# Opening loads of a gated linear-attention and token-MLP kernel: two x tiles moved to Pool's queue, PE's order adapted to it

## Chip, cores, metric

One core of one Trainium2 chip. The metric is device time in microseconds (us). The kernel before takes 165.78 us (median of 6 runs, 165.58 to 165.94). One execution of each kernel was also profiled. Its span, 163.6 us for the kernel before, runs from the first to the last recorded instruction and is some 2 us shorter than the device time. Times inside an execution count from the start of the span.

Engine names are those of the profile: PE (TensorE), PEld (its weight loads), DVE (VectorE), ACT (ScalarE), POOL (GpSimd), SP (SyncE). SP, ACT and Pool can each issue DMA. A queue of one of these engines carries a "q" (SPq). In the DMA parts of the profile, q1 hardware_dynamic is SP's queue, q10 is ACT's, and q0 software_dynamic is Pool's.

## The reference

Condensed from the full program:

```python
def reference(A_x, A_wqkv, A_wo, B_x, B_w1, B_b1, B_w2, B_b2, gate_w):
    x = A_x                                            # 1 x 2048 x 512, bf16
    g = sigmoid((x * gate_w).sum(-1, keepdims=True))
    a = linear_attention(x, A_wqkv, A_wo)              # 32 heads of 16
    b = token_mlp(layernorm(x), B_w1, B_b1, B_w2, B_b2)  # mixes over S, F = 1792
    return g * a + (1 - g) * b
# linear_attention: q, k, v = x @ wqkv; phi(t) = where(t > 0, t + 1, exp(t)) + 1e-6;
# kv = phi(k)^T v; z = sum phi(k); o = phi(q) kv / (phi(q) z); o @ wo
```

## The kernel before

x is cut into 16 tiles of 128 rows. The first stage computes K = x Wk tile by tile, and PE needs x transposed for that. Tiles 4 to 15 arrive transposed by DMA (`load_xT`). Tiles 0 to 3 arrive plain and are transposed by PE, so that work can start early. Wk arrives in four chunks of 128 rows, one per `k`.

```python
    load_x(nc.sync, 0, 1)
    load_x(nc.scalar, 1, 1)
    load_wk(nc.sync, 0)
    load_x(nc.scalar, 2, 1)
    load_x(nc.sync, 3, 1)
    for k, q in ((1, nc.scalar), (2, nc.sync), (3, nc.scalar)):
        load_wk(q, k)
    load_xT(4, 2)
    load_xT(6, 2)
    load_x(nc.sync, 4, 4)
    # ... (cut: the other x tiles, Wq, the w1 chunks, Wv, Wo, all on SP)

    nc.gpsimd.memset(ident[:], 0.0)           # identity for PE's transposes, built on Pool
    nc.gpsimd.affine_select(out=ident[:], ...)
    # ... (cut: two masks on Pool)
    warm_up(6)                                # six matmuls on constants, while x is on its way

    HEADS = 4
    transpose_tile(0, False)                  # 4 PE transposes, then a copy on DVE
    transpose_tile(1, True)                   # the same, copy on ACT
    transpose_tile(2, False)
    ln_step(0)
    for k in range(2):                        # six K matmuls on tiles 0 to 2
        for t in range(HEADS - 1):
            k_part(t, (k,))
    transpose_tile(HEADS - 1, True)           # tile 3
    ln_step(1)
    for t in range(HEADS):
        k_part(t, range(2 if t < HEADS - 1 else 0, ND))
        k_phi(t)
```

PE executes its instructions in this order. If one waits, all behind it wait: in the changed kernel below PE idles 2.63 us for one tile while matmuls on three other tiles stand behind the wait.

## Time and profile before

| | before |
|---|---|
| device time, median | 165.78 us |
| PE busy | 159.9 of 163.6 us |
| x0, x1, x2, x3 landed at | 3.37, 3.54, 4.38, 5.70 us |
| first K matmul starts | 4.82 us |
| last PE matmul starts | 160.55 us |
| last output lands | 162.65 us |
| end of span | 163.61 us |

Landings and starts of single instructions are read from the trace.

From the page of the kernel before: the span, the engines' busy times, PE and DMA in 40 slices (tenths busy), and the chain of waits by engine.

```profile
span 163.6 us, 2078 instructions
PE 159.9 (98%) x785; PEld 73.6 (45%) x785; DVE 87.8 (54%) x200; ACT 58.7 (36%) x90; POOL 18.3 (11%) x37
...
PE   7999999999999999999999999999999999999993
...
DMA  5999999999930005800993499932010000111001
...
PE 98%; DVE 0%; issue 0%
```

PE is busy in every slice and the chain is PE alone. The DMA engines are full in the first slices, so loads compete there.

The timeline of PE in the opening of the kernel before (start, length, then what ran; matmuls of one kind are merged):

```profile
3.42 1.62 PE L194 MATMUL pt<-ident,xs 128*128 128x128 bf16 x12
4.82 1.94 PE L108 MATMUL kacc<-wk_sb,xT 128*128 128x512 bf16 x6
6.60 0.39 PE L194 MATMUL pt<-ident,xs 128*128 128x128 bf16 x4
6.83 3.19 PE L108 MATMUL kacc<-wk_sb,xT 128*128 128x512 bf16 x14
```

(The view ends at 13 us.) No line carries an idle time in brackets; a pause of 0.18 us before tile 2's transposes is merged into the first line. Tile 3 landed at 5.70 us and was transposed at 6.60: the six K matmuls in the second line hid its arrival. The fourth line has 14 matmuls in 3.19 us, one every 0.216 us. The first two of the second line started 0.43 us apart. That is the spacing until PE's granted clock rises; this trace holds no clock record.

### The profile page before, as it was taken

To read this page: it belongs to the slowest core of one execution; us is meant where nothing else is said; L and a number is where in the kernel's file an instruction comes from. 1 tells how busy PE (TensorE), PEld (TensorE's weight loads), DVE (VectorE), ACT (ScalarE), POOL (GpSimd) and SP (SyncE) were. 2 spreads that over 40 slices of the span, in tenths; PEclk is the share of its full clock that TensorE was granted. 3 is DMA by queue.
4 is the path that set the end of the run, shared out by engine and by line. 5 is a ranking of instruction groups with operands and counts; after the bars stand their busy time and mean duration, and the time that the engine had idled before them with its cause. 6 is when DMAs were issued, how large, how long until landed. Compare 5 with 4: busy or idle time off the path is not lost.

```text
span 163.6 us, 2078 instructions
## 1 busy us (share of the span) xinstructions
PE 159.9 (98%) x785; PEld 73.6 (45%) x785; DVE 87.8 (54%) x200; ACT 58.7 (36%) x90; POOL 18.3 (11%) x37
## 2 busy tenths in 40 slices
PE   7999999999999999999999999999999999999993
PEld 3444444444544444434444444444444444444452
DVE  0599999958999999109995301156221111111112
ACT  3463386658478373311332113111112222211110
POOL 5000710200200000001055500050000000000000
DMA  5999999999930005800993499932010000111001
GB/s 152 242 243 236 294 300 344 349 348 348 317 78 0 0 0 188 264 0 0 277 303 109 149 289 307 337 126 98 32 36 32 32 32 32 42 50 41 32 32 32
DMA packets 30057, 25.05 MB, mean 153 GB/s; under 512 B 7968, under 2 KB 29472, under 8 KB 30048
## 3 DMA queue, kind: packets, MB, share of 16 engines
q1 hardware_dynamic: 28032, 22.02, 45.5%
q0 software_dynamic: 1440, 2.38, 5.4%
q10 hardware_dynamic: 576, 0.52, 1.1%
q8 instruction: 6, 0.10, 0.2%
q14 instruction: 3, 0.02, 0.0%
HBM read 21.11 MB, written 2.23 MB: 143 GB/s over the span
## 4 chain that ended last, share of the span: by engine, by line
PE 98%; DVE 0%; issue 0%
PE uacc L108 30%; PE yps L108 30%; PE kacc L108 9%; PE aps L108 8%; PE qacc L108 8%; PE gacc L108 8%; PE wps L108 2%; PE pt L194 1%; PE denps L108 1%; PE kvps L108 1%; DVE ot L474 0%; PE zps L108 0%; PE pt L323 0%
## 5 line engine op out<-in xcount | busy, mean ns | idle before, releaser
L108 PE MATMUL uacc<-hs,w1c 128*128 128x512 bf16 x224 | 52.1, 379 | 0.0
L108 PE MATMUL yps<-uT,w2c 128*128 128x512 bf16 (+2 forms) x238 | 51.0, 366 | 0.0
L474 DVE SCALAR_TENSOR_TENSOR ot<-yps,c,a_sc 128x512 bf16<-128x512 f32 (+2 forms) x17 | 12.2, 720 | 45.9 <-PE yps L108 45.8
L108 PEld LDWEIGHTS <-w2c 128*128 128x128 bf16 x238 | 22.8, 98 | 25.9
L108 PEld LDWEIGHTS <-w1c 128*128 128x128 bf16 x224 | 21.7, 98 | 26.0 <-issue 0.4
L461 ACT ACTIVATE a_sc<-aps,c,gg 128x512 f32<-128x512 f32 x16 | 12.4, 778 | 46.7 <-PE aps L108 43.0
L317 ACT ACTIVATE uT<-uacc,bcol 128x512 bf16<-128x512 f32 x14 | 9.3, 687 | 27.7 <-PE uacc L108 27.7
L108 PE MATMUL aps<-W2sb,pqT 128*128 128x512 bf16 x64 | 16.4, 379 | 0.0
L108 PE MATMUL qacc<-xT,wq_sb 128*128 128x512 bf16 x64 | 16.4, 379 | 0.0
L108 PE MATMUL kacc<-wk_sb,xT 128*128 128x512 bf16 x64 | 16.4, 385 | 0.0
L108 PE MATMUL gacc<-pk,xs 128*128 128x512 bf16 x64 | 15.8, 379 | 0.0
L244 ACT ACTIVATE hs<-xs,nmr,rstd 128x512 bf16<-128x512 bf16 x16 | 12.8, 805 | 1.9 <-DVE nmr L238 1.9
L204 ACT ACTIVATE e<-qacc 128x512 bf16<-128x512 f32 x16 | 9.6, 597 | 10.1 <-PE qacc L108 9.2
L413 POOL DMA_DIRECT2D rex<-rd_dram x16 | 9.5, 603 | 23.0 <-DVE pqT L415 18.2
L204 ACT ACTIVATE e<-kacc 128x512 bf16<-128x512 f32 x16 | 9.3, 595 | 6.9 <-PE kacc L108 6.8
L208 DVE SCALAR_TENSOR_TENSOR pk<-kacc,e 128x512 bf16<-128x512 f32 x16 | 11.1, 692 | 0.6
L208 DVE SCALAR_TENSOR_TENSOR pqT<-qacc,e 128x512 bf16<-128x512 f32 x16 | 11.1, 692 | 0.6
L228 DVE BATCH_NORM_STATS2 stats<-xs 128x6 f32<-128x512 bf16 x16 | 10.9, 682 | 0.0
L205 DVE TENSOR_SCALAR e<-e 128x512 bf16<-128x512 bf16 x32 | 9.0, 282 | 3.3 <-ACT e L204 3.3
L400 DVE CUSTOM_DVE_ANT_0 junk<-xs,gw_b 128x512 bf16<-128x512 bf16 x16 | 9.8, 685 | 0.0
L269 DVE TENSOR_TENSOR zacc<-zacc,pk 128x512 f32<-128x512 f32 x14 | 9.6, 686 | 0.2
L108 PEld LDWEIGHTS <-wq_sb 128*128 128x128 bf16 x64 | 6.3, 98 | 7.5
(64 smaller groups left out, 70.1 us busy)
## 6 DMA issues: line engine op xcount, KB each, us to landing
w2c<-in_B_w_dram SPq DMA_DIRECT2D x8, 896.0 KB, 7.5
w1c<-in_B_w_dram SPq DMA_DIRECT2D x2, 2048.0 KB, 15.5
w1c<-in_B_w_dram SPq DMA_DIRECT2D x3, 1024.0 KB, 12.3
rex<-rd_dram POOLq DMA_DIRECT2D x16, 128.0 KB, 2.9
out_dram<-ot SPq DMA_DIRECT2D x15, 128.0 KB, 1.7
xs<-in_A_x_dram SPq DMA_DIRECT2D x3, 512.0 KB, 4.5
wq_sb<-in_A_wqkv_dram SPq DMA_DIRECT2D x1, 512.0 KB, 6.8
wv_sb<-in_A_wqkv_dram SPq DMA_DIRECT2D x1, 512.0 KB, 12.3
```

What stands on the lines that cost most here:

```text
L108: nc.tensor.matmul(o, lhsT=lhsT, rhs=rhs, start=start, stop=stop, **kw)
L204: nc.scalar.activation(out=e[:], in_=acc[:], func=ACT.Exp)
L205: nc.vector.tensor_scalar(out=e[:], in0=e[:], scalar1=1.0, scalar2=PHI_EPS, op0=ALU.min, op1=ALU.add)
L208: nc.vector.scalar_tensor_tensor(out=dst, in0=acc[:], scalar=0.0, in1=e[:], op0=ALU.max, op1=ALU.add)
L228: nc.vector.bn_stats(out=stats[:], in_=xs[:, t, :])
L244: nc.scalar.activation(out=hs[:, t, :], in_=xs[:, t, :], func=ACT.Identity, scale=rstd[:, t : t + 1], bias=nmr[:, t : t + 1],)
L269: nc.vector.tensor_tensor(out=zacc[:], in0=first, in1=pk[:, t, :], op=ALU.add)
L317: nc.scalar.activation(out=uT[:, j, :], in_=acc[:], func=ACT.Gelu_apprx_tanh, bias=bcol[:, j : j + 1])
L400: nc.vector.tensor_tensor_reduce(out=junk[:], in0=xs[:, t, :], in1=gw_b[:], scale=1.0, scalar=0.0, op0=ALU.mult, op1=ALU.add, accum_out=gp ...
L413: nc.gpsimd.dma_start(out=rex[:], in_=src.unsqueeze(1).to_broadcast([8, HEAD, SC]))
L461: nc.scalar.activation(out=a_sc[:], in_=aps[:], func=ACT.Identity, scale=gg[:, t : t + 1], bias=c2[:, t : t + 1],)
L474: nc.vector.scalar_tensor_tensor(out=ot[:, :W], in0=yps[:, :W], scalar=c1[:, t : t + 1], in1=a_sc[:, cs], op0=ALU.mult, op1=ALU.add,)
```

## The change

The intent is to get the opening loads out sooner by using a third queue. x2 and x3 go to Pool's queue, so SP and ACT carry only x0, x1 and Wk. PE then transposes all four tiles before any K matmul, and the w1 chunks 1 and 2 are loaded in halves.

```diff
     load_x(nc.sync, 0, 1)
     load_x(nc.scalar, 1, 1)
-    load_wk(nc.sync, 0)
-    load_x(nc.scalar, 2, 1)
-    load_x(nc.sync, 3, 1)
-    for k, q in ((1, nc.scalar), (2, nc.sync), (3, nc.scalar)):
+    load_x(nc.gpsimd, 2, 1)
+    for k, q in enumerate((nc.sync, nc.scalar, nc.sync, nc.scalar)):
         load_wk(q, k)
@@ (w1 chunks)
-        for t0 in range(0, NT, 8) if c == 0 else (0,):
-            t1 = t0 + 8 if c == 0 else NT
+        for t0 in range(0, NT, 8) if c < 3 else (0,):
+            t1 = t0 + 8 if c < 3 else NT
@@ (after the identity is built on Pool)
+    load_x(nc.gpsimd, 3, 1)
     block_mask(mask[:]...)
@@ (PE's order)
     ln_step(0)
+    transpose_tile(3, True)
+    ln_step(1)
     for k in range(2):
-        for t in range(HEADS - 1):
+        for t in range(HEADS):
             k_part(t, (k,))
-    transpose_tile(HEADS - 1, True)
-    ln_step(1)
     for t in range(HEADS):
-        k_part(t, range(2 if t < HEADS - 1 else 0, ND))
+        k_part(t, range(2, ND))
         k_phi(t)
```

## The prediction

> **What bounds the kernel now.** TensorE. The page has PE busy 98% of a 163.6 us span, and the chain that ended last is 98% PE. In the timeline, matmuls of 512 columns start every 216 ns from about 6.0 us to the last one at 160 us; beyond that spacing I find only some 0.4 us. Only the first 6 us are in play.
>
> There, by the timeline and the DMA landings: x tiles 0 and 1 are issued at 0.80 us and land at 3.4 and 3.5; six warm-up matmuls fill PE from 0.84 to 3.4. Twelve transposes follow at 107 ns each (to 4.8 us), with one pause of 0.18 us for tile 2 (ACT's second DMA, issued 1.24, landed 4.38). Then six K matmuls hide the wait for tile 3 (issued 1.73, landed 5.70), which is transposed at 6.60. Spacing halves (427 to 216 ns) at about 5.6 us: PE is cold before. Real idle in the opening is about 0.25 us.
>
> **What the change does.**
> - x2 goes out on Pool at about 0.8 us. Pool issues in this trace take 0.6 us and land 2.65 us after their start when the queues are quiet: 3.5 to 3.9 us. The 0.18 us pause goes.
> - Pool's identity is built 0.6 us later, about 2.0 us; needed at 3.4. Free.
> - x3 goes out on Pool behind it, at about 2.0 us, later than before (1.73). Pool DMAs beside a bulk load took 3.8 to 4.1 us, and the loads issued around 2 us here 4.0 to 4.6. Estimate: landing at 5.3 to 6.3 us, no sooner than before.
> - The Wk chunks go out up to 0.5 us earlier; none was waited for.
> - SP's first transposing load waits until 3.55 us because its semaphore is that of x tile 1. With two loads fewer on SP and ACT I expect it at 2.2 us, its traffic meeting x3's. The Trainium skill ("DMA: Bandwidth & Descriptors", section "Issuing engines are not separate DMA queues") says all queues share the same 16 engines; DMA is already above 90% busy from 2.5 us here.
> - Tile 3's transpose now stands before all K matmuls. After 12 transposes (4.7 us) it must wait for x3: 0.6 to 1.6 us idle where before six K matmuls ran.
> - Split w1 chunks: before, they land by 48 us and are used later. No gain.
>
> **Sum.** Before, the dense stream starts as if at 6.83 - 6 x 0.216 = 5.53 us; after, at x3's landing plus 0.25: 5.55 to 6.55. That is 0 to +1.0 us. The idle may also hold the clock down: the skill ("TensorE: Matmul & The Clock Gate", Part 1) gives a free-running activity window of about 3.4 us. If the window that ended near 5.4 us no longer counts as busy, PE stays cold up to 3 us longer, costing up to 1.5 us (estimate). I give this one chance in three.
>
> **Prediction.** 166.4 us, 80% range 165.2 to 167.9. Faster by over 2%: 0.01; within 2%: 0.95; slower by over 2%: 0.04.
>
> **What would show it.** A PE wait of 0.6 us or more at the transposes of tile 3, ended by the x DMA; x3 landing after 5.3 us; no pause before tile 2's transposes; the first transposing load issued near 2.2 us; the spacing change at 5.6 us or up to 3 us later; nothing new after 10 us.
>
> **What would make it wrong.** x3 landing before 4.8 us would gain about 0.5 us. Pool's first DMA slowing x0 and x1 would shift everything. A landing after 7 us would exceed the range.

## More of the kernel before

The DMA view of the kernel before (what was loaded, issuing queue, count, KB each, median us from issue to landing), in two stretches: the x tiles issued in the first 3 us, and Pool's loads issued from 17.6 to 19 us, when the DMA engines were full:

```profile
xs<-in_A_x_dram ACTq DMA_DIRECT2D x2, 128.0 KB, 2.9
xs<-in_A_x_dram SPq DMA_DIRECT2D x2, 128.0 KB, 3.3
...
gw_b<-in_gate_w_dram POOLq DMA_DIRECT2D x1, 128.0 KB, 6.9
brow<-in_B_b_dram POOLq DMA_DIRECT2D x1, 3.5 KB, 6.3
brow<-in_B_b_dram POOLq DMA_DIRECT2D x1, 4.0 KB, 6.5
```

The last two lines matter later: on Pool's queue even 4 KB took over 6 us when the engines were full.

## The result, and the profile after

The changed kernel takes 170.94 us (median of 6 runs, 169.72 to 172.39; the longest counts as slow and is left out of the ratio) against 165.78: it is slower, by a ratio of 1.030 (95% interval 1.024 to 1.036). All ratios here are the mean time of one kernel's runs over that of the other's in the same rounds, so not quite the ratio of the quoted medians. Executions over 1.5% slower than the fastest of the same kernel are left out of the means. The prediction was 166.4 us, so it was 4.5 us too low.

From the page of the changed kernel, the lines that answer to those above:

```profile
span 169.4 us, 2066 instructions
PE 161.6 (95%) x771; PEld 74.2 (44%) x785; DVE 87.7 (52%) x200; ACT 58.7 (35%) x90; POOL 19.4 (11%) x39
...
PE   7399999999999999999999999999999999999992
...
PE 93%; DMA 3%; issue 1%; POOL 1%; DVE 0%; POOLq 0%
```

PE's second slice (4.2 to 8.5 us) fell from 9 to 3, and DMA entered the chain with 3%. (14 of PE's matmul records are missing from this trace.) The timeline of PE in the same opening:

```profile
3.62 1.03 PE L193 MATMUL pt<-ident,xs 128*128 128x128 bf16 x8
4.89 0.61 PE L193 MATMUL pt<-ident,xs 128*128 128x128 bf16 x4 [0.24 <-DMA xs<-in_A_x_dram]
8.14 0.61 PE L193 MATMUL pt<-ident,xs 128*128 128x128 bf16 x4 [2.63 <-DMA xs<-in_A_x_dram]
8.53 4.82 PE L108 MATMUL kacc<-wk_sb,xT 128*128 128x512 bf16 x11
```

PE waits for x2 and then, before the third line, for x3. The last line shows the second loss: 11 K matmuls in 4.82 us, where before 14 took 3.19. They start 0.427 us apart until 12.8 us, and the granted clock rises at 13.15.

The chain of waits of the changed kernel, opening, in order of time (start, us, what):

```profile
1.36 0.71 POOL xs L124
2.08 0.23 POOL ident L162
...
2.37 0.25 POOL ident L163
2.62 5.47 DMA xs<-in_A_x_dram
...
8.14 0.61 PE pt L193 x4
```

The end of the program hangs on x3's landing. Its load was issued at 2.62 us on Pool, behind x2's issue and the identity, and landed 5.47 us later. The same load on SP was issued at 1.73 us before and landed 3.97 us later.

From the DMA view, x tiles issued in the first 3 us of the changed kernel:

```profile
xs<-in_A_x_dram POOLq DMA_DIRECT2D x2, 128.0 KB, 4.5
xs<-in_A_x_dram ACTq DMA_DIRECT2D x1, 128.0 KB, 2.9
xs<-in_A_x_dram SPq DMA_DIRECT2D x1, 128.0 KB, 2.8
```

A ledger of the 5.77 us between the two spans, from start times in the two traces:

| where | before | after | difference |
|---|---|---|---|
| tile 0's transposes start (x0 landed 3.37, then 3.57) | 3.42 | 3.62 | 0.20 |
| pause before tile 2's transposes, beyond the spacing of 0.107 | 0.18 | 0.44 | 0.26 |
| pause before tile 3's transposes, likewise | 0 | 2.84 | 2.84 |
| tile 3's first transpose to the next K matmul (107 ns a transpose, before 55) | 0.22 | 0.40 | 0.18 |
| K matmuls beyond 216 ns each, sum | 0.49 | 2.29 | 1.80 |
| sum of these | | | 5.28 |
| measured: last PE matmul starts | 160.55 | 165.84 | 5.29 |
| measured: last output's landing to end of span | 0.96 | 1.44 | 0.48 |

So there are three losses: a wait for x3, a clock that is still low after the wait, and 0.5 us behind the last output. The stream in between kept its length: from the first gacc matmul (the kind that follows the first K tiles, at 9.85 and 15.14 us) to the last matmul it takes 150.70 to 150.71 us in all fifteen traces. So every difference between these kernels lies in the opening or behind the last matmul.

### The profile page after: what moved, and what is told of

The parts are those of the page before. It is cut to its first block, busy times and chain, and to the rows that moved or that the text cites. A ratio compares the mean times of both kernels' runs of the same rounds, so it can differ in the third digit from the quotient of the medians.

```text
span 169.4 us, 2066 instructions
## 1 busy us (share of the span) xinstructions
PE 161.6 (95%) x771; PEld 74.2 (44%) x785; DVE 87.7 (52%) x200; ACT 58.7 (35%) x90; POOL 19.4 (11%) x39
## 4 chain that ended last, share of the span: by engine, by line
PE 93%; DMA 3%; issue 1%; POOL 1%; DVE 0%; POOLq 0%
PE uacc L108 29%; PE yps L108 28%; PE kacc L108 9%; PE qacc L108 8%; PE gacc L108 8%; PE aps L108 8%; DMA xs<-in_A_x_dram 3%; PE denps L108 1%; PE kvps L108 1%; PE wps L108 1%; POOL xs L124 0%; PE pt L193 0%; DVE ot L473 0%; POOL ident L163 0%; POOL ident L162 0%
## 5 line engine op out<-in xcount | busy, mean ns | idle before, releaser
L108 PE MATMUL kacc<-wk_sb,xT 128*128 128x512 bf16 x63 | 17.8, 422 | 0.0
L243 ACT ACTIVATE hs<-xs,nmr,rstd 128x512 bf16<-128x512 bf16 x16 | 12.8, 804 | 2.3 <-DVE nmr L237 2.3
L108 PEld LDWEIGHTS <-xT 128*128 128x128 bf16 x64 | 6.8, 107 | 9.1 <-issue 2.7
```

Source lines behind the costliest of these rows:

```text
L108: nc.tensor.matmul(o, lhsT=lhsT, rhs=rhs, start=start, stop=stop, **kw)
L243: nc.scalar.activation(out=hs[:, t, :], in_=xs[:, t, :], func=ACT.Identity, scale=rstd[:, t : t + 1], bias=nmr[:, t : t + 1],)
```

## The experiments

Thirteen further programs ran: twelve other kernels and the changed one once more. Two theories stood against each other at the start. Mine was that the transposing loads, issued 1.3 us earlier than before because their semaphore was free, had pushed x3 back in the shared DMA engines, and that the new order exposed this. The rival was that Pool's queue is the slow part by itself. Two cruder rivals were "the order alone" and "the loads alone".

This table collects the profiled run of each. "Cold K" counts K matmuls that started visibly more than 216 ns after the one before; "closing" is the last output's landing to the end of the span. Where "cold K" is 1, that one matmul waited for the copy of its transposed tile (PEld idled 0.53 to 0.58 us for it), so none was cold; one or two of the 2 or 3 in before, w1_split and x2_pool may be of that kind too.

| kernel | median us | ratio to before | x3 issued, on | x3 landed | first K | cold K | closing |
|---|---|---|---|---|---|---|---|
| before | 165.78 | 1 | 1.73 SP | 5.70 | 4.82 | 3 | 0.96 |
| after | 170.94 | 1.030 | 2.62 Pool | 8.09 | 8.53 | 11 | 1.44 |
| after_again | 171.81 | 1.038 | 2.62 Pool | 8.56 | 9.01 | 8 | 1.44 |
| order_back | 168.39 | 1.016 | 2.61 Pool | 9.18 | 6.31 | 1 | 1.45 |
| order_only | 166.77 | 1.007 | 1.73 SP | 5.33 | 5.61 | 1 | 0.96 |
| xT_held | 170.63 | 1.030 | 2.63 Pool | 7.43 | 7.87 | 13 | 1.85 |
| x3_on_act | 168.87 | 1.019 | 2.21 ACT | 6.18 | 6.46 | 1 | 1.90 |
| warm_fill | 170.55 | 1.030 | 2.62 Pool | 9.69 | 9.97 | 1 | 1.45 |
| pool_first | 169.39 | 1.021 | 2.05 Pool | 6.62 | 6.90 | 1 | 1.44 |
| hw_light2 | 168.81 (1 run) | | 2.62 Pool | 6.09 | 6.54 | 7 | 1.67 |
| x4_ahead | 171.34 | 1.033 | 2.62 Pool | 8.37 | 8.82 | 9 | 1.44 |
| pool_one | 169.37 | 1.023 | 1.34 Pool | 6.79 | 7.67 | 5 | 1.45 |
| w1_split | 166.55 | 1.004 | 1.75 SP | 5.68 | 4.87 | 3 | 1.85 |
| no_split | 171.53 | 1.026 | 2.62 Pool | 6.90 | 7.35 | 6 | 1.28 |
| x2_pool | 166.81 | 1.009 | 1.75 SP | 5.56 | 5.31 | 2 | 1.06 |

The profiled run is one run, and x3's landing on Pool varies from run to run, so a median need not match the trace of its row. no_split's trace (device time 168.95 us) is well below its other runs. Five of these kernels have exactly the opening loads of the changed one (after, after_again, order_back, warm_fill, no_split), and x3 landed between 6.90 and 9.69 us in them. A single landing inside that range says nothing of an edit.

### order_back and order_only: the order of PE's work

order_back (from the changed kernel):

```diff
-    transpose_tile(3, True)
-    ln_step(1)
     for k in range(2):
-        for t in range(HEADS):
+        for t in range(HEADS - 1):
             k_part(t, (k,))
+    transpose_tile(HEADS - 1, True)
+    ln_step(1)
     for t in range(HEADS):
-        k_part(t, range(2, ND))
+        k_part(t, range(2 if t < HEADS - 1 else 0, ND))
```

> The changed kernel, with the transposes of tile 3 put back behind the first six K matmuls as in the kernel before. Theory (order exposes a late x3, and the idle holds the clock down): x3 still lands near 8.1 us; PE runs six K matmuls from about 5.3 us, so the wait at tile 3 shrinks from 2.6-2.9 us to about 0.3-1.4 us (the shorter if they run cold at 427 ns), the dense stream ends up about 6 matmuls x 0.216 = 1.3 us earlier, and if the clock rises by about 9 us instead of 13 us another 1 to 2 us come back: 167 to 169 us. Rival A (the order is all of it): 165.8 us as before. Rival B (loads alone, order irrelevant): 171 us unchanged.

order_only is the kernel before with the same hunk the other way round.

> The kernel before with only the order of PE's work changed (tile 3 transposed ahead of all K matmuls); loads as before. Theory: x3 lands at 5.7 us as before, PE idles from about 4.8 to 5.7 us (0.9 us), the stream is 0.3 to 0.6 us later; if that shorter idle already keeps the clock low until about 9 us, up to 1.7 us more: 166.1 to 168 us. Rival A (the order is all of it): 171 us. Rival B (loads alone): 165.8 us.

Measured: order_back 168.39 us (ratio 1.016, interval 1.014 to 1.018), order_only 166.77 us (1.007, interval 1.002 to 1.013). Neither the order nor the loads are all of it. The timeline of PE in order_back:

```profile
6.08 0.40 PE L193 MATMUL pt<-ident,xs 128*128 128x128 bf16 x4 [1.60 <-DMA xs<-in_A_x_dram]
6.31 1.72 PE L108 MATMUL kacc<-wk_sb,xT 128*128 128x512 bf16 x6
9.23 0.40 PE L193 MATMUL pt<-ident,xs 128*128 128x128 bf16 x4 [1.20 <-DMA xs<-in_A_x_dram]
9.46 3.19 PE L108 MATMUL kacc<-wk_sb,xT 128*128 128x512 bf16 x14
```

x3 landed at 9.18 us here, later than in the changed kernel, and yet the run was 2.6 us shorter (168.81 against 171.44 us for the two profiled runs). Six K matmuls ran inside the wait, and the 14 after it ran at full speed. The second part is not owed to the order: the granted clock rose at 3.99 us here, before PE's order differs from the changed kernel's, and it stayed up through both waits. Here x2 was late as well (1.60 us waited). In order_only the wait for tile 3 came to 0.35 us by the profile (this view ends at 8 us):

```profile
3.49 1.53 PE L194 MATMUL pt<-ident,xs 128*128 128x128 bf16 x12
5.37 0.40 PE L194 MATMUL pt<-ident,xs 128*128 128x128 bf16 x4 [0.35 <-DMA xs<-in_A_x_dram]
5.61 2.75 PE L108 MATMUL kacc<-wk_sb,xT 128*128 128x512 bf16 x11
```

What follows: with x3 on time the new order costs about 1 us on average (runs from 165.75 to 168.11); with x3 late it also gives up the only work that could hide the lateness.

### xT_held and x3_on_act: what makes x3 late

xT_held delays the transposing loads to where they were before, by two tiny loads that take up the free semaphores:

```diff
+    fill = keep([NT, 2 * P], BF16, "fill")
+    b2_rows = B_b2.rearrange("(f q) -> f q", q=P)
+    nc.sync.dma_start(out=fill[:, 0:P], in_=b2_rows)
+    nc.scalar.dma_start(out=fill[:, P : 2 * P], in_=b2_rows)
     load_xT(4, 2)
```

> The changed kernel with two tiny loads (4 KB each) put in front of the first transposing load, so that its semaphore is again that of x tile 1 and it is issued at about 3.8 us instead of 2.21. Theory (the transposing loads, let go 1.3 us earlier, are what x3's packets queue behind): x3 lands at 5.9 to 6.6 us instead of 8.1, PE's wait at tile 3 is 0.7 to 1.3 us, time 167 to 169 us. Rival C (Pool's software queue and its late issue at 2.62 us are the cause by themselves): x3 lands at 7.5 us or later, and the time stays at 170 to 172 us.

x3_on_act moves only x3, to another queue and with that to an earlier issue:

```diff
+    load_x(nc.scalar, 3, 1)      # behind Wk chunk 3
     load_xT(4, 2)
...
-    load_x(nc.gpsimd, 3, 1)      # behind the identity
```

> The changed kernel with x tile 3 as the last of ACT's loads (issued at about 2.2 us, behind Wk chunks 1 and 3) instead of on Pool; x2 stays on Pool, the transposing loads stay early at 2.2 and 3.6 us. Theory (transposing loads ahead of it in the shared engines): x3 lands at 6.8 us or later, time 168 to 171 us. Rival C (Pool's queue is the slow part): x3 lands like a late ACT load of before, at 6.3 us or sooner, and the time falls to 166.5 to 168 us.

Measured: with the transposing loads held to 3.53 us (2.21 before the hold), x3 landed at 7.43 us and the time stayed at 170.63 us (ratio 1.030). With the transposing loads early and x3 on ACT, x3 landed at 6.18 us and the time fell to 168.87 us (1.019). The DMA view and the chain of x3_on_act:

```profile
xs<-in_A_x_dram ACTq DMA_DIRECT2D x1, 128.0 KB, 4.0
...
2.21 3.97 DMA xs<-in_A_x_dram
...
6.23 0.40 PE pt L193 x4
```

And the chain of xT_held, with its two tiny loads in the DMA view:

```profile
2.63 4.80 DMA xs<-in_A_x_dram
...
7.47 0.61 PE pt L197 x4
...
fill<-in_B_b_dram SPq DMA_DIRECT2D x1, 4.0 KB, 5.0
fill<-in_B_b_dram ACTq DMA_DIRECT2D x1, 4.0 KB, 5.2
```

My theory missed: with the transposing loads held back x3 did not land at 5.9 to 6.6 us, and the time stayed (x3's 7.43 us lies inside the range of the changed kernel's loads). Moving x3 to ACT did gain time, beside the same early transposing loads. But x3_on_act does not isolate Pool's queue, as I took it to do: x3 was also issued at 2.21 us instead of 2.62. And xT_held speaks against a queue that is slow by itself: two loads of 4 KB, issued at 2.2 us on SP and ACT, took 5.0 and 5.2 us there, Pool's x3 4.8. x3_on_act was not as fast as its rival's 166.5 to 168 us. In its trace x2 still waited on Pool (landed 4.85 us) and the order still exposed x3.

### pool_first, hw_light2, x4_ahead, pool_one: Pool's queue

> The changed kernel with both Pool loads ahead of building the identity, so x3 is issued at about 2.1 us instead of 2.62. Theory now (Pool's queue is served late and slowly beside busy SP and ACT queues): x3 lands 4.5 to 6.5 us after its issue still, at 6.6 to 8.6 us; time 169.5 to 171.5 us. Rival (the late issue behind the identity is the cause): x3 lands at about 5.3 to 6.0 us, time 167 to 168.5 us.

```diff
     load_x(nc.gpsimd, 2, 1)
+    load_x(nc.gpsimd, 3, 1)
...
-    load_x(nc.gpsimd, 3, 1)      # behind the identity
```

> The changed kernel with four tiny loads (2 KB each) after Wk chunk 1, so that Wk chunks 2 and 3 and the transposing loads must wait for the semaphores of x0, x1 and the loads behind them (issued near 3.6 us or later). Until then only x0, x1, two Wk chunks and Pool's two x tiles are in flight. Only x3's landing counts. Theory (contention with the other two queues): x3 lands 2.7 to 3.5 us after its issue at 2.6, at 5.3 to 6.2 us. Rival (Pool's queue is slow by itself in the opening): x3 lands at 7.2 us or later.

```diff
-    for k, q in enumerate((nc.sync, nc.scalar, nc.sync, nc.scalar)):
-        load_wk(q, k)
+    load_wk(nc.sync, 0)
+    load_wk(nc.scalar, 1)
+    # (cut) four loads of 2 KB, alternating SP and ACT
+    load_wk(nc.sync, 2)
+    load_wk(nc.scalar, 3)
```

(A first form of this kernel, hw_light, did not build for lack of SBUF. Its tiny loads were 4 KB each.)

> The changed kernel with the plain 512 KB load of x tiles 4 to 7 put ahead of the two transposing loads on SP, so that x3's packets on Pool's queue share the engines with plain 1 KB packets and not with the 256-byte packets of the transposing loads. If the mixture of Pool's packets with transposing packets is what slows x3: x3 lands at 5.8 to 6.8 us, time 167.5 to 169.5 us. If any full traffic of the other queues slows Pool's: x3 lands at 7.4 us or later as in the changed kernel, 170 to 172 us.

```diff
+    load_x(nc.sync, 4, 4)
     load_xT(4, 2)
     load_xT(6, 2)
-    load_x(nc.sync, 4, 4)
```

> The changed kernel with x2 and x3 in one 256 KB load on Pool, issued at 1.33 us ahead of the identity. If the number and lateness of Pool's issues counts: both tiles land together at 5.5 to 6.6 us, PE waits once for about 1.3 to 2 us, 168 to 170 us. If Pool's second 128 KB is served slowly whatever its issue: landing at 7.5 us or later, 170 to 172 us.

```diff
-    load_x(nc.gpsimd, 2, 1)
+    load_x(nc.gpsimd, 2, 2)
...
-    load_x(nc.gpsimd, 3, 1)      # behind the identity
```

Measured, with x3's time from issue to landing: pool_first 4.57 us (time 169.39), hw_light2 3.47 us (one run, 168.81), x4_ahead 5.75 us (171.34), pool_one 5.45 us for both tiles together (169.37). The chain of pool_first:

```profile
2.05 4.57 DMA xs<-in_A_x_dram
...
6.66 0.40 PE pt L193 x4
```

- hw_light2: with little traffic from SP and ACT, Pool's x3 lands about as fast as a load on SP or ACT. So the traffic counts; x3's issue behind the identity is not enough to explain 8 us.
- x4_ahead: plain traffic ahead delays x3 as much as transposing traffic (8.37 us), so the kind of packet does not decide.
- pool_first and pool_one: an earlier issue, or one issue for both, brings the time down by some 1.5 us (pool_first by 2.4 us against after_again in the same rounds). It does not bring x3 to 5.3 to 6.0 us, as the rival in pool_first's text had it. But it gives back about as much as x3_on_act did: the ratio is 1.021 (interval 1.016 to 1.026) with x3 on Pool issued at 2.05 us, and 1.019 (1.013 to 1.025) with x3 on ACT issued at 2.21. So these runs do not show that it was the change of queue that helped x3_on_act.

The traces show one thing about the queue. Pool's packets start late: x2's first packet moved at 3.50 us in the changed kernel, 2.17 us after its issue began at 1.33, while SP's first packet moved at 1.84 us, 1.03 us after its issue at 0.81. x3's first packet moved at 4.78 us, again 2.16 us after its issue began; that x3 had to wait for x2's packets on the queue is not shown. The DMA view of the stretch from 5 to 8 us, changed kernel (packets and MB in all, then each queue's share of 16 engines' time):

```profile
DMA packets 1586, 0.52 MB, mean 173 GB/s; under 512 B 1548, under 2 KB 1555, under 8 KB 1586
...
q1 hardware_dynamic: 1530, 0.38, 89.7%
q0 software_dynamic: 47, 0.13, 30.2%
```

and x4_ahead:

```profile
DMA packets 1151, 0.83 MB, mean 276 GB/s; under 512 B 568, under 2 KB 1119, under 8 KB 1151
...
q1 hardware_dynamic: 1077, 0.68, 101.2%
q0 software_dynamic: 49, 0.13, 11.9%
```

In both, x3's 0.13 MB needed this stretch, and in both it landed after 8 us. In the changed kernel the engines moved less in all (173 GB/s against 276), in x4_ahead they were fast and x3 waited for its turn: its first packet started at 6.34 us, 3.7 us after its issue. Why the engines give Pool's packets their turn so late is not settled by these runs. (DVE is no likely cause: it was busy for 0.55 us of these 3.7.)

Taken together, x3 is late where its issue comes late among the opening loads and much traffic is about. Before, it was the fifth of eight loads of 128 KB. In the changed kernel it is the last, behind all Wk chunks and one transposing load, and as the last of the eight it lands last on ACT too: in x3_on_act x3 landed at 6.18 us, behind Wk chunks 2 and 3 at 5.38 and 5.95. Loads on SP and ACT can be as late: Wk chunks 2 and 3 took 6.4 and 6.6 us in order_back. What Pool's queue adds by itself is not isolated. No run issued x3 at 2.62 us on another queue.

Over all traces, a 128 KB x3 took 3.5 to 7.1 us to land on Pool (nine traces) and 3.6 to 4.0 us on SP or ACT (five traces).

### after_again and warm_fill: the clock

> The changed kernel unaltered, for a second trace. Its six earlier runs fall into two groups, 169.7 to 170.4 us (mean granted clock 0.99) and 171.4 to 172.4 us (1.0). Theory (the phase of the clock's activity window decides how many K matmuls run at 427 ns): again two groups about 1.7 us apart; x3 lands anywhere from 7.4 to 9.2 us, as in the runs so far. Rival (the two groups come from the landing of x3): the groups follow x3's landing, and a trace of the faster group has x3 1.7 us earlier.

> The changed kernel with six of the warm-up matmuls repeated between the transposes of tile 2 and tile 3, where PE only waits. Loads unchanged, results unchanged. Theory (idle plus cold clock): the wait for x3 stays, but the clock is granted by about 7 us and never taken back, so the K matmuls after tile 3 run at 216 ns: 1.5 to 2.3 us less than the changed kernel, 168 to 169.5 us, and the two groups of run times close up. Rival (the wait alone costs the 5 us): 171 us unchanged, or slower by what the fill costs.

```diff
+    warm_up(6)
     transpose_tile(3, True)
```

The K matmuls of the changed kernel, from the view of their tile between 8.7 and 12.5 us, with minimum, median and maximum length in ns:

```profile
L108 PE MATMUL kacc<-wk_sb,xT x10: 634/634/634, 8.5 to 12.4; 128*128 128x512 bf16 x10
```

and the same window of the kernel before:

```profile
L108 PE MATMUL kacc<-wk_sb,xT x12: 379/379/379, 8.3 to 12.4; 128*128 128x512 bf16 x12
```

In warm_fill the same wait was filled with matmuls on constants. Its timeline:

```profile
6.28 2.77 PE L108 MATMUL wps<-const-bfloat16-1.0 128*128 128x512 bf16 x6
9.74 0.40 PE L193 MATMUL pt<-ident,xs 128*128 128x128 bf16 x4 [0.70 <-DMA xs<-in_A_x_dram]
9.97 4.69 PE L108 MATMUL kacc<-wk_sb,xT 128*128 128x512 bf16 x20
```

x3 landed at 9.69 us here, the latest of all, but no K matmul was cold and the median came down to 170.55 us from 171.81 us for after_again in the same rounds. That is 1.3 us, short of the expected 1.5 to 2.3. The clock loss is therefore separate from the wait. In the records the granted clock starts at 13.15 us in the changed kernel, 12.16 in after_again, 9.59 in warm_fill, and 4 to 6 us in order_back, order_only, x3_on_act, pool_first, x2_pool and w1_split. In order_back (3.99) and pool_first (4.25) PE had done the same work until then as in the changed kernel, and waits of up to 1.6 us afterwards did not lower the clock. So chance has a part in whether the cold matmuls come at all, and a part of what these two gained in the profiled run.

The two groups of run times that I had seen in the first six runs did not come again: after_again gave 171.20, 171.79, 171.84 and 172.66 us. That the phase of the clock's window makes two groups is not shown.

### w1_split and no_split: behind the last output

> The kernel before with only the split of the w1 chunks 1 and 2 into two loads each. All of them land many us before they are used: 165.6 to 165.9 us, no difference. If the time moves by over 0.3 us, the split is a part of the change's effect after all.

```diff
-        for t0 in range(0, NT, 8) if c == 0 else (0,):
-            t1 = t0 + 8 if c == 0 else NT
+        for t0 in range(0, NT, 8) if c < 3 else (0,):
+            t1 = t0 + 8 if c < 3 else NT
```

w1_split came out at 166.55 us, 0.4% slower (interval 0.2 to 0.6%), where I had expected nothing. PE's last matmul starts at 160.66 us in it, against 160.55 before. The time is lost behind the last output: 1.85 us from its landing to the end of the span instead of 0.96. SP closes the program by waiting for all DMA semaphores, two at a time in a fixed order. In the trace of the kernel before, the last output's semaphore is in the ninth and last of these waits, so the others are over when it lands. In w1_split two loads more on SP have shifted the round of semaphores: it is in the third, and the six waits after it run afterwards, to 0.45 us past the landing. Another 0.46 us pass before SP's next drain. That second pause is also in the changed kernel (drain at 0.56 us past the landing instead of 0.15); its cause is not known.

> The changed kernel without the split of the w1 chunks 1 and 2. The split alone cost 0.7 us on the kernel before, and its trace put that behind the last output: from the last output's landing to the end of the program 1.85 us instead of 0.96 (the changed kernel: 1.44). Theory (the number of loads decides which semaphore the last output uses, and SP's closing waits go round them in a fixed order; a longer SP program adds a pause of 0.46 us before SP's drain): without the split the closing part is 0.96 to 1.2 us, and the opening is as bad as ever: 170.4 to 171.4 us. Rival (the split also matters in the middle of the kernel): the stream between 12 and 165 us changes length by over 0.3 us.

no_split is the changed kernel with the hunk above undone. Its closing part is 1.28 us, somewhat over the expected 0.96 to 1.2: two more waits follow that of the last output (0.16 us), and the rest lies in SP's steps behind them. Its runs vary as those of the changed kernel do (168.95 to 172.08 us; two of the four, 171.90 and 172.08, count as slow), so the saving doesn't show in the median of 171.53. The stream from the first gacc matmul to the last matmul did not change.

### x2_pool: one tile on Pool

> The kernel before with only x2 moved to Pool: x3 on SP, the order of PE's work, and the split as before. Theory (Pool's queue lands 3.5 to 4.6 us after its issue at 1.33 us here): x2 lands at 4.85 to 5.9 us instead of 4.38, PE waits 0.5 to 1.5 us for it with nothing else to do, and the K matmuls after it stay warm or nearly: 166.2 to 167.6 us. If a single load on Pool costs nothing, 165.7 us; if any use of Pool in the opening brings the whole loss, 170 us.

```diff
-    load_x(nc.scalar, 2, 1)
+    load_x(nc.gpsimd, 2, 1)
```

This is the kernel before with that line alone changed (the first transposing load then goes out at 2.71 us instead of 3.55): 166.81 us (ratio 1.009, interval 1.002 to 1.016), with single runs from 165.90 to 168.36. In the profiled run, a lucky one of 165.97 us, x2 landed at 4.87 us instead of 4.38. One tile on Pool already costs, and makes the time vary, but it is not the whole loss.

None of these kernels beat the kernel before. After the first x tile has landed its PE idles only for the 0.18 us before tile 2, about 0.1% of its time, so faster loads of the other tiles have little more to give.

## Why the prediction was wrong

- **PE bound, only the opening in play: right** for all but 0.5 us. The last PE matmul shifted by 5.29 us, and 5.28 us are found before 13.2 us.
- **"The 0.18 us pause goes": wrong.** x2 was predicted at 3.5 to 3.9 us and landed at 4.84 (5.85 in the second trace). Pool's first issue began at 1.33 us, not 0.8, and its first packet moved 2.17 us later.
- **"Estimate: landing at 5.3 to 6.3 us": the step that failed.** x3 landed at 8.09 and 8.56 us. I had taken Pool's landing from loads beside one bulk load (3.8 to 4.1 us). The same trace held Pool loads at full DMA traffic with 6.3 to 6.9 us, and the opening has full traffic. The issue was at 2.62 us instead of 2.0, since Pool began x2's issue 0.53 us later than assumed and took 0.74 us for it. So the issue was 0.6 us late, and the landing took 5.47 and 5.95 us from there where I had assumed 3.3 to 4.3. With the measured landing the prediction's own sum gives 8.09 + 0.25 - 5.53 = 2.81 us. The cold matmuls behind the landing (2.29 us of K, 0.18 of transposes) make up the other 2.5 of the 5.29. How x3's extra time from issue to landing divides between Pool's queue, its place behind the other loads and the traffic stays open.
- **"0.6 to 1.6 us idle" at tile 3: right in place, wrong in size.** It was 2.84 us, ended by the x DMA as described.
- **The first transposing load "expected at 2.2 us": right** (2.21). **"Its traffic meeting x3's": not shown to be the cause.** Holding it back left the time as it was; issuing x3 ahead of it (pool_first) helped, but that was also an earlier issue.
- **The clock, "one chance in three", up to 1.5 us: happened, and was under-rated.** It cost 1.80 us on K matmuls, compared with the kernel before, and 0.18 on transposes in the profiled run; in after_again 8 K matmuls were cold. The Trainium skill ("TensorE: Matmul & The Clock Gate", Part 1) gives 426.7 ns between cold matmuls of 512 columns and 215.7 ns between warm ones; the traces show 427 and 216, so page and trace agree.
- **"Split w1 chunks: no gain": right, but they cost.** The split on the kernel before took 0.7 us; in the changed kernel the closing part is 0.48 us longer.
- **"Nothing new after 10 us": wrong** by the cold matmuls up to 12.8 us and by the closing part.

The Trainium skill ("DMA: Bandwidth & Descriptors", section "Issuing engines are not separate DMA queues") says that issuing from several engines only saves the time of the issue. The runs agree and go further: here the third queue gave the tile that PE needed next a later issue and a later landing.

## What to carry to other kernels

A queue is chosen by its landing time under the traffic of that very moment, and that time is often in the trace already: look for loads of the same queue in full slices, not in quiet ones. Look as well at the place of a load in the order of issue over all queues: here x3 went from fifth to last. Before moving a wait ahead of independent work on an in-order engine, add up what a late arrival would cost there, and on PE allow for cold matmuls after the idle too. When a change adds or removes loads, look behind the last output as well, because the closing waits can shift by half a microsecond or more.

## What the Trainium skill lacked or had wrong

- "DMA: Bandwidth & Descriptors", sections "Specifications" and "Latency and other measured facts": about 1 us to the first byte on Pool's path and 0.6 us on SP's and ACT's. In the changed kernel's trace Pool's first packet moved 2.17 us after the start of its issue (which itself took 0.74 us), so 1.43 us after its end, and SP's 1.03 us after the start and 0.63 us after the end. Counted from the end of the issue SP's figure agrees in this trace, and Pool's is low (1.3 to 1.7 us in all twelve traces with an opening load on Pool).
- The same page, "Anatomy of one DMA — SWDGE (gpsimd) path": about 2.0 us plus bytes over 436 GB/s, so an estimate of 2.3 us for 128 KB. x3 took 3.5 us with little other traffic and 4.3 to 7.1 us with the full opening traffic of SP and ACT; the page has no figure for Pool's queue beside busy ones.
- The same page, "Queues, rings and completion order": an engine takes its queues in turn, packet by packet. In x4_ahead x3's first packet started 3.7 us after its issue while SP's queue ran at full rate; these runs don't tell why.
- None of the pages has the waits on DMA semaphores with which the program itself closes: 0.96 to 1.90 us from the last output's landing to the end of the span, partly by the position of the last output's semaphore in SP's fixed round of waits.
